# Linear attention with a bilinear FFN on one core: pair scores by whole 128x128 blocks and the state update as a step of its own

## The chip, the cores and the metric

One core of one Trainium2 chip runs the whole program. The metric is the device time of one execution in microseconds (us). It is a little longer than the span that the profile shows, which runs from the first to the last instruction.

## What is computed

The reference cut to what matters (B=4, H=8, S=768, D=48; x has 3072 tokens of 384 features; d_ff=1024; all in float32 at the end):

```python
f = 1.0 / (1.0 + np.exp(-f_logit))
for t in range(S):
    state = f[:, :, t, :, None] * state + np.einsum('bhd,bhe->bhde', k[:, :, t], v[:, :, t])
    y[:, :, t] = np.einsum('bhd,bhde->bhe', q[:, :, t], state)
x = y.transpose(0, 2, 1, 3).reshape(B * S, H * D)
a = x @ w1
b = x @ w2
h = a * b @ w3
out = h @ w_out
```

The first part is a gated linear attention with a decay per feature, the second an FFN whose hidden layer is the product of two projections.

## The kernel before, in words

**Attention by chunks.** The sequence is cut into NU = 24 chunks of C = 128 tokens, six per batch entry (NCH = 6). A chunk has eight heads as four pairs (HP = 4): the two heads of a pair lie on partitions 0 to 47 and 64 to 111. For chunk u the gate is a sigmoid on ScalarE (L386). Two scans on VectorE make the running products forwards and backwards (L394, L416), and q and k are scaled by them into Q (L410) and K (L431 and L432; the second writes the two halves of 64 tokens of every second pair in swapped places, and v is loaded in three transfers, L349 and L351, so that its rows fit).

**Pairs** (L457, and L445 for the first four chunks): K^T Q per head gives a 128x128 block of scores, laid into the PSUM tile pa. From chunk 4 (NPE = 4) a block is made on 64x64 tiles of the array: the 64 early keys against all 128 queries, and the 64 late keys against the 64 late queries. The quarter in which every key is later than every query isn't computed. There are 16 matmuls in a chunk and 32 instructions, since a float32 matmul is two. The first four chunks use 8 matmuls of 128x128 (16 instructions). ScalarE copies pa into the tile A (L542, three copies in a chunk; L539, one copy, in the first four). GpSimd zeroes what lies beyond the diagonal by affine_select (L548: four selects of 64x256 in a chunk, one of 128x1024 in the first four). In chunks 4 and 5 it also clears the quarters that nothing writes (L559, L560).

**Values** (L490): v^T A per head, into pa again from chunk 4. **Update** (L522): K^T of the chunk, turned by PE transposes (L467, PSUM tile pk) and copied (L567), times v. It isn't made for the last chunk of a batch entry ("closes": 5, 11, 17, 23). VectorE adds the result to the state S (L611 to L617) and ScalarE spreads it into sb (L625). **State** (L509): sb^T Q added onto the values, not for the first chunk of an entry ("opens": 6, 12, 18). From chunk 4 these three make one step of PE: values, update, state, in that order. For the first four chunks, update is a step of its own.

**y.** ScalarE copies y out with its sum (L635). From chunk 4 it is written to memory by features in two transfers (L655) and read back as x^T in one (L658). The first four chunks are permuted on PE instead (L663).

**Weights and FFN.** The weights come as 64-bit words and are turned to float32 on ScalarE and VectorE (L1079 to L1096). w3 and w_out are folded into one matrix on PE (L1143, copied out at L1150). Six blocks of 512 tokens go through the FFN (L685). Its two products use seven multiplications in place of eight on half matrices, with sums on VectorE (L755, L809 to L827, L921 to L970).

**Order of the work.** Nothing is scheduled by the compiler. A planner (class Plan, L74) holds tasks with an engine, a cost, dependencies and a priority. It takes again and again the task that can start first (ties by priority) and so fixes the order of each engine's instructions. Attention from chunk 4 has priorities of n0 - 1000 (pairs), - 999 (turn), - 998 (values), - 997 (update), far ahead of the FFN, and each such PE task adds a slack of 0.8 to what it waits for on another engine. A dependency across engines adds a lag of 0.2. FFN tasks cost 0.43 to 1.33 in the plan, and folds 5.15. PSUM banks of the FFN are five named tiles (plan.pool "f"), taken as they come free. Loads go through moves (L334), which counts each transfer on SP (0.45) and at most eight outstanding ones ("lane").

Of the kernel before, what the change touches and what calls it, by code (L numbers as in the profile page):

```python
# [73 lines left out]
class Plan:  # L74


    def __init__(self):
        self.tasks = []
        self.slots = {}
        self.pools = {}  # L80
        self.got = None

    def slot(self, name, n):

        self.slots[name] = [n, []]

    def pool(self, name, n):

        self.pools[name] = [None] * n
# [11 lines left out]
    def order(self):  # L101
# [6 lines left out]
        def after(t, ds):  # L108

            if any(d["end"] is None for d in ds):  # L110
                return None
            return max([0.0] + [d["end"] + (d["lag"] + t["slack"] if d["eng"] != t["eng"] else 0.0) for d in ds])

        def places(t, name):

            ends = [(after(t, enders[id(h)]) if h else 0.0, i) for i, h in enumerate(self.pools[name])]
            return [e for e in ends if e[0] is not None]

        def start(t):

            waits, at = list(t["deps"]), free.get(t["eng"], 0.0)
            for name in t["takes"]:
                if name in self.pools:
                    ends = places(t, name)
                    if not ends:
                        return None
                    at = max(at, min(ends)[0])
                    continue
                n, taken = self.slots[name]
                if len(taken) >= n:  # L130
                    waits += enders[id(taken[-n])]
            ready = after(t, waits)
            return None if ready is None else max(at, ready)

        while left:
            at, _, _, t = min(
                ((at, t["prio"], t["no"], t) for t in left if (at := start(t)) is not None), key=lambda x: x[:3]
            )
            t["at"], t["end"] = at, at + t["cost"]
            free[t["eng"]] = t["end"]  # L140
            for name in t["takes"]:
                if name in self.pools:
                    t["got"] = min(places(t, name))[1]
                    self.pools[name][t["got"]] = t
                else:
                    self.slots[name][1].append(t)
            left.remove(t)
            done.append(t)
# [57 lines left out]
def ranged(ctx, tc, q, k, f_logit, v, w1, w2, w3, w_out, out, ident, w12, wc, left):  # L206
# [14 lines left out]
    ps_f = ctx.enter_context(tc.tile_pool(name="ps_f", bufs=1, space=PSUM))  # L221
# [5 lines left out]
    masked = [keep.tile([P, 2, HP, C], F32, name=f"A{i}") for i in range(2)]  # L227
# [34 lines left out]
    plan.pool("f", NF)  # L262
    plan.slot("a", 2)
    plan.slot("lane", 8)
# [4 lines left out]
    def bank():  # L269

        return ps_f.tile([P, TB], F32, name=f"f{plan.got}")

    def idle(n):

        to = ps_f.tile([P, TB], F32, name=f"f{NF - 1}")[:, 0:TH]
# [58 lines left out]
    def moves(n, size, rate, emit, deps, prio, late=0.0):  # L334


        for j in range(n):
            i = plan.add("SP", 0.45, (lambda: None) if j else emit, [d] if j else deps, prio - j * 1e-3, takes=["lane"], lag=0.6)
            d = i
            t = plan.add("DMA", size / n / rate, lambda: None, [i], prio - j * 1e-3, lag=1.3 + late, frees=[i])  # L340
        return t

    def loaded(dst, u):

        if u < NPE:
            nc.sync.dma_start(dst, v[u])
            return
        to, of = (t.rearrange("p (b two m) -> p b two m", two=2, m=2 * D) for t in (dst, v[u]))
        nc.sync.dma_start(to[:, :, 0], of[:, :, 0])  # L349
        for a in (0, 64):  # L350
            nc.sync.dma_start(to[a : a + 64, :, 1], of[64 - a : P - a, :, 1])  # L351

    def front(u):

        s, t = st[u], tk[u]
        n0 = need(u)

# [13 lines left out]

        t["lf"] = moves(2, 197, 250, load(fu, f_logit), free(2, "g"), n0 - 30)
        t["lk"] = moves(2, 197, 250, load(ku, k), free(2, "k"), n0 - 29.5)
        t["lq"] = moves(2, 197, 250, load(qu, q), free(3, "q"), n0 - 29)

        def load_v():
            s["v"] = at(12288 + NQ, DM) if u == 3 else loads.tile([P, DM], F32, name="vt")
            loaded(s["v"], u)

        t["lv"] = moves(  # L380
            1 if u < NPE else 3, 197, 320, load_v, [] if u == 3 else past(u, 4 if u in (4, 5, 6) else 3, "v", "s"),
            n0 - (28.2, 28.2, 28.2, 29.6, 12)[min(u, NPE)],
        )
# [5 lines left out]
        if u % NCH and "d" in tk[u - 1]:  # L389
# [32 lines left out]
        def scale_k():  # L422
            s["K"] = work.tile([R, NQ], F32, name="K")
            if u < NPE:
                nc.vector.tensor_tensor(s["K"], ku, s["R"], ALU.mult)
                return

            kk, k_, r_ = (
                x.rearrange("p (b two h c) -> p b two h c", two=2, h=2, c=C // 2) for x in (s["K"], ku, s["R"])
            )  # L430
            nc.vector.tensor_tensor(kk[:, :, 0], k_[:, :, 0], r_[:, :, 0], ALU.mult)  # L431
            nc.vector.tensor_tensor(kk[:, :, 1, ::-1], k_[:, :, 1], r_[:, :, 1], ALU.mult)  # L432

        t["k"] = plan.add("DVE", 0.7 if u < NPE else 0.8, scale_k, [t["r"], t["lk"]] + past(u, 2, "a", "t"), n0)
# [3 lines left out]
    def pairs(u):  # L438
        s = st[u]
        s["pa"] = ps.tile([P, 2, NQ], F32, name="pa")  # L440
        if u < NPE:
# [7 lines left out]
            return  # L449

        for hp in range(0, HP, 2):
            for late in range(2):
                for swap in range(2):
                    a = (hp + swap) * C
                    h0 = 64 * (late ^ swap)
                    for par in range(2):
                        nc.tensor.matmul(  # L457
                            s["pa"][h0 : h0 + 64, par, a + 64 * late : a + C],
                            lhsT=s["K"][rows(par), a + h0 : a + h0 + 64],
                            rhs=s["Q"][rows(par), a + 64 * late : a + C], start=True, stop=True,  # L460
                        )

    def turn(u):
        s = st[u]
        s["pk"] = ps.tile([P, HP, R], F32, name="pk")
        for hp in range(HP):
            nc.tensor.transpose(  # L467
                out=s["pk"][:, hp], in_=s["K"][:, hp * C : hp * C + C],
                identity=ident[0:R, 0:R],
            )  # L470

    def y_block(u, b):
        py = st[u]["py"]
        return py[:, b] if u < NPE else py[0:R, b // 2, b % 2 * C : b % 2 * C + C]

    def values(u):
        s = st[u]
        opens = u % NCH == 0
        if u < NPE:
            s["py"] = bank().rearrange("p (h c) -> p h c", c=C)[0:R]  # L480
        else:
            s["py"] = ps.tile([P, 2, NQ], F32, name="pa")
        met_ = set()
        for hp in heads_of(u):
            for par in range(2):
                h = 2 * hp + par
                half, b = side(u, hp, par)
                w = 64 if half == 0 else D
                zone = (half, 0 if u < NPE else par)
                nc.tensor.matmul(  # L490
                    y_block(u, b)[64 * half : 64 * half + w], lhsT=s["v"][:, h * D : h * D + w],
                    rhs=s["A"][:, par, hp], start=zone not in met_, stop=opens, skip_group_check=True,
                )
                met_.add(zone)

    def from_state(u):
        s = st[u]
        if u % NCH == 0:
            return
        for hp in heads_of(u):  # L500
            if u < NPE:
                nc.tensor.matmul(
                    y_block(u, hp), lhsT=sb[(u - 1) % 2][:, hp], rhs=s["Q"][:, hp * C : hp * C + C],
                    start=False, stop=True, skip_group_check=True,
                )
                continue
            for par in range(2):
                half, b = side(u, hp, par)
                nc.tensor.matmul(  # L509
                    y_block(u, b)[rows(half)], lhsT=sb[(u - 1) % 2][rows(par), hp, rows(par)],  # L510
                    rhs=s["Q"][rows(par), hp * C : hp * C + C], start=False, stop=True,
                    skip_group_check=True,
                )

    def update(u):
        s = st[u]
        s["pd"] = ps.tile([P, HP, R], F32, name="pk")[0:R, :, 0:D]
        for hp in range(HP):
            for par in range(2):
                h = 2 * hp + par  # L520
                w = 64 if par == 0 else D
                nc.tensor.matmul(  # L522
                    s["pd"][64 * par : 64 * par + w, hp], lhsT=s["kt"][:, hp, 64 * par : 64 * par + w],
# [1044 lines left out]
```

## Time and profile before

| | us |
|---|---|
| median of 3 runs (lowest to highest) | 499.08 (499.04 to 499.2) |
| the profiled execution, its own time | 499.08 |
| its span | 497.2 |
| PE busy | 484.9 |
| VectorE busy | 362.1 |
| ScalarE busy | 166.8 |
| GpSimd busy | 69.7 |
| mean granted TensorE clock | 0.998 |

The rows of the trace give the start of an instruction (or of a run of like instructions), its length, its engine and line, the tiles as out<-in, and in brackets how long the engine had been idle and what ended that. Matmuls overlap in the array, so the time that one costs is the distance from its start to the start of the next, not its own length. The times of the rows count from the start of the span. The stages are: chunks 0 to 3 and the start (0 to 36 us), the first FFN block, the weights and the fold (to 135 us), chunks 4 to 23 among FFN work (83 to 314 us), and the rest of the FFN (to 494 us).

### The profile page before, as it was taken

To read this page: it belongs to the slowest core of one execution; us is meant where nothing else is said; L and a number is where in the kernel's file an instruction comes from. 1 tells how busy PE (TensorE), PEld (TensorE's weight loads), DVE (VectorE), ACT (ScalarE), POOL (GpSimd) and SP (SyncE) were. 2 spreads that over 40 slices of the span, in tenths; PEclk is the share of its full clock that TensorE was granted. 3 is DMA by queue.
4 is the path that set the end of the run, shared out by engine and by line. 5 is a ranking of instruction groups with operands and counts; after the bars stand their busy time and mean duration, and the time that the engine had idled before them with its cause. 6 is when DMAs were issued, how large, how long until landed. Compare 5 with 4: busy or idle time off the path is not lost.

```text
span 497.2 us, 9542 instructions
## 1 busy us (share of the span) xinstructions
PE 484.9 (98%) x3698; PEld 407.6 (82%) x3698; DVE 362.1 (73%) x721; ACT 166.8 (34%) x380; POOL 69.7 (14%) x115
## 2 busy tenths in 40 slices
PE   8889999999999999999999999999999999999995
PEld 6778745655799888889888888998899888889994
DVE  7998899989989677878677965446673667664541
ACT  4688456662433444443334443101100111101000
POOL 9210000432212111123212221000000000000000
PEclk9999999999999999999999999999999999999999
DMA  6889377563335554344532203100021000000011
GB/s 177 293 301 280 98 248 257 194 180 96 96 98 142 153 147 100 99 120 138 139 86 74 55 18 82 48 33 0 2 63 49 16 1 0 1 0 2 32 55 48
DMA packets 44789, 49.99 MB, mean 101 GB/s; under 512 B 15296, under 2 KB 34240, under 8 KB 43712
## 3 DMA queue, kind: packets, MB, share of 16 engines
q1 hardware_dynamic: 44736, 49.30, 33.3%
q8 instruction: 31, 0.51, 0.4%
q14 instruction: 22, 0.18, 0.1%
HBM read 40.63 MB, written 8.65 MB: 99 GB/s over the span
## 4 chain that ended last, share of the span: by engine, by line
PE 76%; POOL 1%; DVE 0%; ACT 0%; issue 0%
PE f L685 61%; PE pa L490 4%; PE f L1143 3%; PE pa L457 3%; PE pa L509 2%; PE pk L467 2%; PE pk L522 1%; POOL A L548 0%; ACT ys L635 0%; DVE place L949 0%; DVE o L970 0%; POOL A L560 0%; POOL A L559 0%; DVE nil L1202 0%; DVE zero L1200 0%
## 5 line engine op out<-in xcount | busy, mean ns | idle before, releaser
L685 PE MATMUL f<-xt,w 128*128 128x256 f32 (+1 forms) x600 | 158.5, 396 | 0.0
L685 PEld LDWEIGHTS f<-xt,w 128*128 128x128 f32 x600 | 113.6, 190 | 24.9 <-issue 11.2
L685 PE MATMUL f<-place 128*128 128x192 f32 (+1 forms) x504 | 112.6, 350 | 0.0
L685 PEld LDWEIGHTS f<-place 128*128 128x128 f32 x504 | 87.5, 190 | 6.1 <-DVE place L809 0.5
L548 POOL TENSOR_SCALAR_AFFINE_SELECT A<-A 64x256 f32<-64x256 f32 (+1 forms) x84 | 57.2, 701 | 239.2 <-PE pk L467 104.3
L1143 PE MATMUL f<-place 128*128 128x384 f32 x128 | 43.1, 490 | 0.6 <-ACT wc L1150 0.6
L788 ACT COPY a<-f 128x256 f32<-128x256 f32 x36 | 13.4, 372 | 77.4 <-PE f L685 67.2
L685 PE MATMUL f<-xt,place 128*128 128x256 f32 x144 | 37.7, 385 | 0.0
L1143 PEld LDWEIGHTS f<-place 128*128 128x128 f32 x128 | 23.8, 190 | 17.0 <-ACT wc L1150 1.2
L685 PE MATMUL f<-wc,ab 128*128 128x192 f32 x192 | 35.4, 327 | 0.0
L685 PEld LDWEIGHTS f<-wc,ab 128*128 128x128 f32 x192 | 31.9, 190 | 0.7 <-issue 0.4
L394 DVE TENSOR_TENSOR_SCAN fwd<-gate,floor 112x512 f32<-112x512 f32 x24 | 29.7, 1237 | 2.6 <-ACT gate L386 2.1
L416 DVE TENSOR_TENSOR_SCAN bwd<-gate,back 112x512 f32<-112x512 f32 x24 | 29.4, 1226 | 0.7
L812 DVE TENSOR_TENSOR place<-f,a 128x256 f32<-128x256 f32 x36 | 15.2, 423 | 20.2 <-PE f L685 20.2
L685 PEld LDWEIGHTS f<-xt,place 128*128 128x128 f32 x144 | 26.4, 189 | 4.0 <-issue 0.4
L542 ACT COPY A<-pa 64x256 f32<-64x256 f32 (+1 forms) x60 | 24.3, 439 | 13.9 <-PE pa L457 13.3
L635 ACT ACTIVATE ys<-pa 112x512 f32<-112x512 f32 x20 | 11.9, 597 | 49.9 <-PE pa L509 45.7
L490 PEld LDWEIGHTS pa<-A,vt 128*64 128x64 f32 (+1 forms) x320 | 17.6, 129 | 7.8 <-issue 5.5
L490 PE MATMUL pa<-A,vt 128*64 128x128 f32 (+1 forms) x320 | 22.7, 280 | 1.0 <-POOL A L560 1.0
L1079 ACT ACTIVATE place<-place 128x512 f32<-128x512 f32 (+2 forms) x24 | 21.2, 884 | 3.5 <-DVE w L1096 2.0
L685 PE MATMUL f<-place,w 128*128 128x256 f32 x72 | 21.6, 382 | 0.0
L1082 ACT ACTIVATE place<-place 128x512 f32<-128x512 uint32 (+2 forms) x24 | 21.1, 885 | 0.0
(117 smaller groups left out, 638.6 us busy)
## 6 DMA issues: line engine op xcount, KB each, us to landing
place<-in_w_dram SPq DMA_DIRECT2D x8, 1024.0 KB, 4.8
place<-in_w_dram SPq DMA_DIRECT2D x12, 512.0 KB, 9.3
out_dram<-o SPq DMA_DIRECT2D x24, 192.0 KB, 1.9
q<-in_q_dram SPq DMA_DIRECT2D x46, 96.0 KB, 2.4
f<-in_f_logit_dram SPq DMA_DIRECT2D x44, 96.0 KB, 2.4
k<-in_k_dram SPq DMA_DIRECT2D x44, 96.0 KB, 2.3
yt<-ys SPq DMA_DIRECT2D x40, 96.0 KB, 2.2
xt<-yt SPq DMA_DIRECT2D x20, 192.0 KB, 2.9
```

Of the source, the lines that this page charges most:

```text
L394: nc.vector.tensor_tensor_scan(s["P"], gate[u % 2][:, 0:NQ], floor, 0.0, ALU.mult, ALU.max)
L416: nc.vector.tensor_tensor_scan(s["R"][:, ::-1], gate[u % 2][:, NQ:0:-1], back[:, ::-1], 0.0, ALU.mult, ALU.max)
L457: nc.tensor.matmul(s["pa"][h0 : h0 + 64, par, a + 64 * late : a + C], lhsT=s["K"][rows(par), a + h0 : a + h0 + 64], rhs=s["Q"][rows(par), ...
L490: nc.tensor.matmul(y_block(u, b)[64 * half : 64 * half + w], lhsT=s["v"][:, h * D : h * D + w], rhs=s["A"][:, par, hp], start=zone not in ...
L542: nc.scalar.copy(parts_of(s["A"].rearrange("p r h c -> p (r h c)"))[p0:p1, :, f], parts_of(s["pa"].rearrange("p r n -> p (r n)"))[p0:p1, : ...
L548: nc.gpsimd.affine_select(out=a, in_=a, pattern=pattern, compare_op=ALU.is_ge, fill=0.0, base=0, channel_multiplier=-1,)
L685: nc.tensor.matmul(out_, lhsT=lhs[i], rhs=rhs[i], start=start and i == 0, stop=i == len(lhs) - 1, skip_group_check=True,)
L788: nc.scalar.copy(q["a"], q["X"])
L812: nc.vector.tensor_tensor(ups["u3", k], q["Y"], q["a"], ALU.add)
L1079: nc.scalar.activation(m, hi.bitcast(F32), AF.Abs)
L1082: nc.scalar.activation(lo.bitcast(F32), lo, AF.Copy, bias=2.0, scale=2.0**-51)
L1143: nc.tensor.matmul(w3s["p", jc], lhsT=w3s[jc][:, kc * P : kc * P + P], rhs=wos[:, kc], start=(kc == 0), stop=(kc == KF - 1),)
```

## The change

From chunk 4 on, the pairs are made as in the first four chunks: eight matmuls of 128x128 in place of sixteen on 64x64 tiles, with one copy on ScalarE in place of three, one select on GpSimd in place of four, and no clearing. K is scaled in one instruction in its natural order, and v is loaded in one transfer in place of three. The state update is again a PE task of its own (cost 0.6, priority n0 - 997), and values with state another. In the planner, the banks "f" are a ring of five taken in turn and not named tiles, a transfer's limit of eight outstanding ones is gone, loads are one task each, the load of v has an earlier priority, and two waits of FFN tasks are moved (takes_ab to c11, got to got0 in down). The FFN's instructions and the way of y through memory (L655, L658) are the same on both sides.

```diff
-        self.pools = {}
-        self.got = None
...
-        def places(t, name):
-
-            ends = [(after(t, enders[id(h)]) if h else 0.0, i) for i, h in enumerate(self.pools[name])]
-            return [e for e in ends if e[0] is not None]
...
-    ps_f = ctx.enter_context(tc.tile_pool(name="ps_f", bufs=1, space=PSUM))
+    ps_f = ctx.enter_context(tc.tile_pool(name="ps_f", bufs=NF, space=PSUM))
...
-    plan.pool("f", NF)
+    plan.slot("f", NF)
     plan.slot("a", 2)
-    plan.slot("lane", 8)
...
-    def moves(n, size, rate, emit, deps, prio, late=0.0):
-
-
-        for j in range(n):
-            i = plan.add("SP", 0.45, (lambda: None) if j else emit, [d] if j else deps, prio - j * 1e-3, takes=["lane"], lag=0.6)
-            d = i
-            t = plan.add("DMA", size / n / rate, lambda: None, [i], prio - j * 1e-3, lag=1.3 + late, frees=[i])
-        return t
+    def moves(issue, size, rate, emit, deps, prio, late=0.0):
+
+        i = plan.add("SP", issue, emit, deps, prio, lag=0.6)
+        return plan.add("DMA", size / rate, lambda: None, [i], prio, lag=1.3 + late)
...
-            loaded(s["v"], u)
-
-        t["lv"] = moves(
-            1 if u < NPE else 3, 197, 320, load_v, [] if u == 3 else past(u, 4 if u in (4, 5, 6) else 3, "v", "s"),
-            n0 - (28.2, 28.2, 28.2, 29.6, 12)[min(u, NPE)],
-        )
+            nc.sync.dma_start(s["v"], v[u])
+
+        t["lv"] = moves(0.45, 197, 320, load_v, [] if u == 3 else past(u, 4 if u in (4, 5, 6) else 3, "v", "s"), n0 - (28.2, 28.2, 28.2, 29.6, 27)[min(u, NPE)])
...
-            kk, k_, r_ = (
-                x.rearrange("p (b two h c) -> p b two h c", two=2, h=2, c=C // 2) for x in (s["K"], ku, s["R"])
-            )
-            nc.vector.tensor_tensor(kk[:, :, 0], k_[:, :, 0], r_[:, :, 0], ALU.mult)
-            nc.vector.tensor_tensor(kk[:, :, 1, ::-1], k_[:, :, 1], r_[:, :, 1], ALU.mult)
+            nc.vector.tensor_tensor(s["K"], ku, s["R"], ALU.mult)
...
-        for hp in range(0, HP, 2):
-            for late in range(2):
-                for swap in range(2):
-                    a = (hp + swap) * C
-                    h0 = 64 * (late ^ swap)
-                    for par in range(2):
-                        nc.tensor.matmul(
-                            s["pa"][h0 : h0 + 64, par, a + 64 * late : a + C],
-                            lhsT=s["K"][rows(par), a + h0 : a + h0 + 64],
-                            rhs=s["Q"][rows(par), a + 64 * late : a + C], start=True, stop=True,
-                        )
...
+        t["a"] = plan.add("PE", 1.1, pairs, [t["q"], t["k"]] + past(u, 1, "y" if u > NPE else "m"), n0 - 1000, slack=slack)
+
+        def taken():
+            s["A"] = work.tile([P, 2, HP, C], F32, name="A")
+            nc.scalar.copy(s["A"].rearrange("p r h c -> p r (h c)"), s["pa"])
+
+        t["m"] = plan.add("ACT", 1.1, taken, [t["a"]] + past(u, 2, "v"), n0)
...
+        t["c"] = plan.add("POOL", 1.2, causal, [t["m"]], n0)
+
+        if not closes:
...
+            t["t"] = plan.add("PE", 0.45, turn, [t["k"]] + past(u, 1, "d"), n0 - 999, slack=slack)
...
-            def value():
-                values(u)
-                if not closes:
-                    update(u)
-                from_state(u)
-
-            t["v"] = t["s"] = plan.add(
-                "PE", 1.2 + 0.35 * (not closes) + 0.5 * (not opens), value,
-                [t["c"], t["lv"]] + past(u, 0, "e") + past(u, 1, "y", "b", "d"), n0 - 998, slack=0.8,
-            )
...
+        t["v"] = plan.add(
+            "PE", 1.05 if opens else 2.1 if u < NPE else 1.6, value, [t["c"], t["lv"]] + past(u, 1, "y", "b"),
+            n0 - 998, takes=["f"] if u < NPE else [], slack=slack,
+        )
...
+            t["s"] = plan.add("PE", 0.6, update, [t["e"], t["lv"]] + past(u, 1, "d"), n0 - 997, slack=slack)
...
-            begin = takes_ab(jc, plan.add("PE", 0.0, lambda: None, ready + [s["S", 3]] + old(1, "m7"), n0))
-            pe("m1", one_, m1, [begin], 0, takes=["f"])
+            pe("m1", one_, m1, ready + [s["S", 3]] + old(1, "m7"), 0, takes=["f"])
...
-                q["c11"] = plan.add("ACT", 0.38, c11, [q["m2"]], -200, frees=[q["m1"]])
+                q["c11"] = takes_ab(jc, plan.add("ACT", 0.38, c11, [q["m2"]], -200, frees=[q["m1"]]))
...
-            pe("m1", m1, got + old("m7"), takes=["f"])
+            pe("m1", m1, got0 + old("m7"), takes=["f"])
```

## The prediction

> **What bounds the kernel now.** I read the page first: busy time, then the waits, then the chain that ended last, in order of time, and last the timeline of PE with its neighbours.
>
> ```profile
> PE 484.9 (98%) x3698; PEld 407.6 (82%) x3698; DVE 362.1 (73%) x721; ACT 166.8 (34%) x380; POOL 69.7 (14%) x115
> ```
>
> TensorE (PE) is busy for all but 12.3 us, and most of those lie in the first 36 us (latency of the first chunks) and after 494 us (the last stores). A busy PE isn't PE at its peak, so I check with the distances between matmuls: from 36.66 us on, matmuls of one shape follow each other at one constant step (8 of 128x192 in 1.30 us below), and PE loses only a few waits. So whatever PE issues more from chunk 4 on lengthens the run by as much, whatever it issues less shortens it, and what ScalarE, VectorE, GpSimd or the DMAs save counts only where PE waits for it. The chain shows what one chunk costs:
>
> ```profile
> 155.17 0.83 PE pa L457 x32
> 156.00 0.54 PE pk L467 x4
> 156.53 5.21 PE f L685 x30
> 161.74 1.06 PE pa L490 x12
> 162.80 0.41 PE pk L522 x13
> 163.21 0.58 PE pa L509 x16
> 163.79 2.79 PE f L685 x14
> ```
>
> Start, length, line: pairs 0.83, turn 0.54, FFN as a filler, then values, update and state in one block of 1.06 + 0.41 + 0.58 = 2.05, and FFN again. (Some matmul records are merged away, so the counts are low. The times aren't.)
>
> **Pairs.** The new form runs in the first four chunks of this same execution:
>
> ```profile
> 9.03 1.16 PE L445 MATMUL pa<-Q,K 48*128 48x128 f32 x16
> 10.12 0.67 PE L522 MATMUL pk<-vt,kt 128*64 128x48 f32 x16
> 10.71 2.43 PE L277 MATMUL f<-floor 112*128 112x256 f32 x10
> ```
>
> From start to start, 8 pairs matmuls of 48x128 (16 instructions) take 10.12 - 9.03 = 1.09 us, and the three other chunks give 1.09 too. Against 0.83 that is +0.26 in each of the 20 chunks from 4 on: **+5.2 us**. Nothing hides it, since PE is what is full.
>
> **Update as a step of its own.** Here it takes 10.71 - 10.12 = 0.59 and not the 0.41 that it adds inside the block. What the array pays for a change from FFN matmuls to the attention's and back is in these rows:
>
> ```profile
> 146.25 1.46 PE L685 MATMUL f<-wc,ab 128*128 128x192 f32 x8
> 147.55 1.46 PE L685 MATMUL f<-place 128*128 128x192 f32 x8
> 148.85 1.46 PE L685 MATMUL f<-place,ab 128*128 128x192 f32 x8
> 150.25 1.13 PE L490 MATMUL pa<-A,vt 128*64 128x128 f32 x16
> 152.30 1.57 PE L685 MATMUL f<-wc,place 128*128 128x192 f32 x8
> 153.70 1.46 PE L685 MATMUL f<-wc,ab 128*128 128x192 f32 x8
> ```
>
> Eight of these take 1.30 (147.55 to 148.85), but 1.40 ahead of the values (148.85 to 150.25) and 1.40 again as the first ones behind them (152.30 to 153.70): 0.10 in, 0.10 out, 0.20 for each separate block. Chunks that make no update show values and state alone: 1.06 + 0.58 (chain, 183.25 and 249.50 us). So a chunk with an update costs, against 2.05 now: about 2.05 where the planner sets the update just ahead of the values (the same shapes in another order, +0); 1.06 + 0.58 + 0.59 = 2.23 where just behind (+0.18); and 1.06 + 0.58 + 0.59 + 0.20 = 2.43 where FFN work lies between (+0.38). By the plan's own numbers the update can start 0.2 + 1.1 + 0.55 + 0.2 + 0.8 = 2.85 us after the pairs (the copy of A, then that of kt, on ScalarE), the values 0.2 + 1.1 + 0.2 + 1.2 + 0.2 + 0.8 = 3.7 after them (copy, select). FFN tasks of 0.43 to 1.33 set the places between, and the turn may come earlier than the pairs now that it no longer follows the values of the chunk before. I can't tell which of the three cases will be most frequent, so I weigh them 0.35, 0.25 and 0.4: 0.25 x 0.18 + 0.4 x 0.38 = 0.20 a chunk. 16 chunks of the 20 have an update: **+3.2 us**, with 0 and 16 x 0.38 = 6.1 as ends.
>
> **Copy, select, clearing.** A chunk's three copies take 1.24 us in a row on ScalarE, the one copy of the first chunks 1.01 (L539). Four selects of 681 ns on the mean give 2.7 us, one of 128x1024 takes 1.11 on the mean. This matters at two places only:
>
> ```profile
> 91.21 4.51 POOL L548 TENSOR_SCALAR_AFFINE_SELECT A<-A 64x256 f32<-64x256 f32 x4 [61.10 <-issue]
> 96.12 0.31 POOL L560 MEMSET A<- 64x256 f32 x1
> 96.48 1.19 PE L490 MATMUL pa<-A,vt 128*64 128x128 f32 x16 [0.66 <-POOL A L560]
> 110.50 1.19 PE L490 MATMUL pa<-A,vt 128*64 128x128 f32 x16 [0.35 <-POOL A L560]
> ```
>
> In chunks 4 and 5 PE stood idle for 0.66 and 0.35 until GpSimd had selected and cleared. With one select and no clearing A is ready about 90.04 + 0.1 + 1.0 + 1.1 to 3 = 92 to 94, ahead of the end of the fold at 95.7: **-1.0 us**. In the chunks after these, FFN work covers the select, and a shorter one gains nothing.
>
> The long select could hurt VectorE:
>
> ```profile
> 12.18 1.09 POOL L548 TENSOR_SCALAR_AFFINE_SELECT A<-A 128x1024 f32<-128x1024 f32 x1
> 12.27 1.54 DVE L425 TENSOR_TENSOR K<-k,bwd 112x512 f32<-112x512 f32 x1
> ```
>
> K took 1.54 beside this select and 0.69 elsewhere, 0.85 more. A rule speaks against the change here: by the Trainium skill, "SBUF — State Buffer", section "Who interferes with whom", GpSimd and VectorE share one port pair under an exclusive lock held for a whole instruction, so one long select may block VectorE's two-input operations for its full length, where a short one lets them in between. By that rule alone, with VectorE as the bound, 20 chunks would lose up to 20 x 1.1 = 22 us, an estimate. I take 0: the four short selects hold VectorE back as well, and between 150 and 200 us VectorE is busy for 40.2 of 50 us and PE for 50.0, so a VectorE that is 0.85 late is caught up. Without that cover the row gives at most 20 x 0.85 = 17 us.
>
> **The rest.** One K instruction of 0.69 stands for two that together take 0.67 from start to next start (140.71 to 141.38): 0. v comes in one transfer for three, which takes two issues a chunk off SP. No values matmul waits for a DMA in the list of waits, so the gain is 0, and VectorE's waits for x^T bound what a worse order of the transfers could cost now that the plan doesn't count eight of them: two waits, 4.4 us in all (DVE L755), 0 of which reach PE today. Taken 0, ends 0 and +4.4. A ring of banks instead of named ones makes a task wait for the oldest bank. In both FFN forms the banks are freed in the order in which they were taken, so I take 0. The nearest wait is PE's 0.6 for a fold's bank (L1143 on L1150), and one of these in each of six blocks would be +3.6. The first 36 us have the same instructions in nearly the same order: 0, with its PE waits of 1.41 at 30 us and 0.8 at 14 us as the ends of a luckier or worse order (-1.5 to +1.5).
>
> **Sum.** 5.2 + 3.2 - 1.0 = +7.4 us on the profiled execution, which took 499.08 us around a span of 497.2; that is also the median of the runs. **Forecast: 506.5 us**, own range 504 to 509.5.
>
> **Rivals.**
> - *New PE waits* (509.5 to 515 us, at 511.6 with 6.1 in place of 3.2 for the updates and half of the 4.4 for the transfers): the plan now knows less of transfers, and its shorter attention loop presses more of VectorE's work into less time. For it: VectorE is over 80% busy where attention runs. Against it: PE shows no such wait between 125 and 300 us, and a slower PE gives VectorE more room.
> - *Only the pairs count* (501.5 to 504 us, at 502.8: 5.2 - 1.0, and -0.5 from the start): updates lie next to the values nearly always. For it: both become ready within 0.85 us. Against it: the update no longer waits for the values' select.
> - *Faster than before* (under 498.1): the shorter chain through ScalarE and GpSimd, 0.2 + 1.6 us less a chunk, pulls PE's waits out. Its place is PE's idle time in the attention stage. It would have to be worth more than 5.2 us. All the waits that I find, from the 0.8 and 1.41 at the start through 0.6 at a fold and 1.0 in chunks 4 and 5 to 0.3 at the last check, are 4.1 us. Removing every one of them gives 499.08 + 5.2 - 4.1 = 500.2, so it decides only if the plan also packs the blocks closer than now. I see nothing that would.
> - *It doesn't do what its title says*: y's three transfers a chunk (L655 twice, L658) stand on both sides of the diff, so nothing comes from there either way. Then the terms above are all there is, and the forecast stays.
>
> **Chances.** Forecast's case 0.58, new waits 0.22, only the pairs 0.14, within 0.2% (a measurement of this kernel can't tell less from no change) 0.03, faster 0.03. So faster 0.03, same 0.03, slower 0.94. The range reaches into both neighbouring cases: 502 to 512.
>
> **What would show it.** L-rows for pairs with 48*128 in all chunks, 1.09 from start to start; update rows of 0.59 with FFN on both sides or next to values; no clearing on GpSimd, 24 selects, and no PE wait for GpSimd at 96 and 110 us; the stage from 317 us on as long as before (some 180 us). I am wrong if the FFN tail changes its length, if PE shows waits of its own between 125 and 314 us, or if the first FFN matmul moves far from 36.66 us.

## The result and the profile after

The changed kernel takes 504.25 us (median of four runs, 504.02 to 505.59) against 499.14 us for the kernel before on the same chip (499.04 to 499.23). The ratio is 1.0108, with a 95% interval of 1.009 to 1.0126: about 1% slower. The profiled execution took 504.48 us around a span of 502.7.

The page of the changed kernel, busy time by engine:

```profile
PE 493.0 (98%) x3378; PEld 411.3 (82%) x3378; DVE 364.1 (72%) x701; ACT 162.1 (32%) x340; POOL 43.7 (9%) x51
```

GpSimd lost 26 us of work and ScalarE 4.7, and the run became longer all the same, because TensorE (PE) got 8.1 us more and still has no room. The chain of waits that ended last (start, length, line; L388 is now the pairs, L414 the turn, L438 the values, L453 the state, L474 the update, L554 the FFN):

```profile
159.41 1.50 PE f L554 x8
160.91 0.59 PE pk L474 x14
161.50 1.49 PE f L554 x6
163.00 1.09 PE pa L388 x16
...
174.26 1.09 PE pa L388 x16
175.35 0.59 PE pk L474 x14
175.95 2.35 PE f L554 x10
178.30 0.39 PE pk L414 x4
178.69 1.31 PE f L554 x6
180.00 1.06 PE pa L438 x13
181.06 0.58 PE pa L453 x16
181.65 0.59 PE pk L474 x14
```

Pairs cost 1.09 where they cost 0.83. The update costs 0.59 where it cost 0.41 inside the block, and it stands in three places here: alone among FFN work (160.91), behind the pairs (175.35), and behind the state (181.65). The turn, which followed the pairs before, often stands by itself (178.30).

Chunks 4 and 5, where PE waited 0.66 and 0.35 us for GpSimd. PE first, then GpSimd:

```profile
88.54 5.34 PE L1011 MATMUL f<-place 128*128 128x384 f32 x16
93.81 1.13 PE L438 MATMUL pa<-A,vt 128*64 128x128 f32 x16
94.87 0.65 PE L453 MATMUL pa<-Q,sb 48*48 48x128 f32 x16
95.45 0.67 PE L474 MATMUL pk<-vt,kt 128*64 128x48 f32 x16
```

```profile
89.35 1.83 POOL L403 TENSOR_SCALAR_AFFINE_SELECT A<-A 128x1024 f32<-128x1024 f32 x1 [60.56 <-ACT A L397]
103.75 1.49 POOL L403 TENSOR_SCALAR_AFFINE_SELECT A<-A 128x1024 f32<-128x1024 f32 x1 [12.57 <-ACT A L397]
```

The first select ends at 91.18, and the values follow the fold of w3 and w_out at 93.81; those of chunk 5 start at 107.85, with the select done at 105.24. No wait stands ahead of the values any more.

The start of the FFN on PE moved:

```profile
29.33 1.13 PE L246 MATMUL f<-floor 112*128 112x256 f32 x4
...
32.37 2.84 PE L532 MATMUL f<-ys,ab 112*128 112x128 f32 x24
35.05 2.32 PE L554 MATMUL f<-xt,w 128*128 128x256 f32 x10
```

The first FFN matmul starts at 35.05 and not at 36.66, and the first fold at 76.37 and not at 77.98. These 1.6 us are a gain.

**Where the time went.** I add up the distances from start to start of PE's matmuls by kind, from the first FFN matmul to the last one, for both profiled executions:

| us | before | after | difference |
|---|---|---|---|
| first FFN matmul | 36.66 | 35.05 | -1.61 |
| pairs (20 chunks) | 16.58 | 21.84 | +5.26 |
| values (20) | 19.10 | 20.97 | +1.87 |
| update (16) | 8.71 | 9.42 | +0.71 |
| turn (16) | 7.07 | 6.78 | -0.29 |
| state | 9.93 | 9.93 | 0 |
| fold, with the waits in it | 44.35 | 42.60 | -1.75 |
| FFN | 348.96 | 349.99 | +1.02 |
| from the last matmul to the end of the span | 5.7 | 6.0 | +0.3 |
| sum | | | +5.5 |

The span grew by 502.7 - 497.2 = 5.5. The -1.75 are three waits that are gone: 0.71 and 0.40 for GpSimd, worked out from the starts, and 0.63 at the second fold.

### The profile page after: what moved, and what is told of

The parts are those of the page before. It is cut to its first block, busy times and chain, and to the rows that moved or that the text cites. A ratio compares the mean times of both kernels' runs of the same rounds, so it can differ in the third digit from the quotient of the medians.

```text
span 502.7 us, 8691 instructions
## 1 busy us (share of the span) xinstructions
PE 493.0 (98%) x3378; PEld 411.3 (82%) x3378; DVE 364.1 (72%) x701; ACT 162.1 (32%) x340; POOL 43.7 (9%) x51
## 2 busy tenths in 40 slices
DMA packets 36466, 49.94 MB, mean 99 GB/s; under 512 B 4416, under 2 KB 25920, under 8 KB 35392
## 4 chain that ended last, share of the span: by engine, by line
PE 95%; DVE 3%; DMA 0%; issue 0%; ACT 0%; POOL 0%; SPq 0%; DVEq 0%; ACTq 0%; POOLq 0%
PE f L554 69%; PE f L1011 8%; PE pa L388 5%; PE pa L438 4%; PE pk L474 2%; PE pa L453 2%; PE pk L414 2%; PE f L532 1%; DVE bwd L369 1%; DVE fwd L347 1%; PE f L446 1%; PE f L438 1%; DVE K L377 0%; DMA f<-in_f_logit_dram 0%; DVE Q L363 0%
## 5 line engine op out<-in xcount | busy, mean ns | idle before, releaser
L554 PE MATMUL f<-xt,w 128*128 128x256 f32 (+1 forms) x600 | 160.2, 398 | 0.0
L554 PEld LDWEIGHTS f<-xt,w 128*128 128x128 f32 x600 | 112.7, 190 | 25.1 <-issue 10.7
L554 PE MATMUL f<-place 128*128 128x192 f32 (+1 forms) x504 | 114.2, 351 | 0.0
L554 PEld LDWEIGHTS f<-place 128*128 128x128 f32 x504 | 87.4, 190 | 6.3 <-issue 0.6
L403 POOL TENSOR_SCALAR_AFFINE_SELECT A<-A 128x1024 f32<-128x1024 f32 x24 | 32.6, 1356 | 251.6 <-ACT A L397 251.6
L554 PE MATMUL f<-xt,place 128*128 128x256 f32 x144 | 37.6, 383 | 0.0
L554 PE MATMUL f<-wc,ab 128*128 128x192 f32 x192 | 35.3, 327 | 0.0
L397 ACT COPY A<-pa 128x1024 f32<-128x1024 f32 x24 | 24.3, 1013 | 28.4 <-PE pa L388 28.4
L347 DVE TENSOR_TENSOR_SCAN fwd<-gate,floor 112x512 f32<-112x512 f32 x24 | 31.1, 1294 | 2.5 <-ACT gate L339 1.7
L554 PEld LDWEIGHTS f<-wc,ab 128*128 128x128 f32 x192 | 32.0, 190 | 0.7 <-issue 0.2
L369 DVE TENSOR_TENSOR_SCAN bwd<-gate,back 112x512 f32<-112x512 f32 x24 | 30.8, 1283 | 0.7
L554 PEld LDWEIGHTS f<-xt,place 128*128 128x128 f32 x144 | 26.6, 189 | 3.9 <-issue 0.2
L388 PEld LDWEIGHTS pa<-Q,K 48*128 48x128 f32 x384 | 23.3, 187 | 7.7 <-issue 4.5
L388 PE MATMUL pa<-Q,K 48*128 48x128 f32 x384 | 27.9, 285 | 0.0
L363 DVE TENSOR_TENSOR Q<-q,fwd 112x512 f32<-112x512 f32 x23 | 16.7, 726 | 10.1 <-PE pa L453 10.1
L798 ACT COPY place<-f 128x192 f32<-128x192 f32 x12 | 3.8, 319 | 61.5 <-PE f L554 39.9
L438 PEld LDWEIGHTS pa<-A,vt 128*64 128x64 f32 (+1 forms) x320 | 17.5, 129 | 6.5 <-issue 6.4
```

Of the source, the lines that this page charges most:

```text
L347: nc.vector.tensor_tensor_scan(s["P"], gate[u % 2][:, 0:NQ], floor, 0.0, ALU.mult, ALU.max)
L363: nc.vector.tensor_tensor(s["Q"], qu, s["P"], ALU.mult)
L369: nc.vector.tensor_tensor_scan(s["R"][:, ::-1], gate[u % 2][:, NQ:0:-1], back[:, ::-1], 0.0, ALU.mult, ALU.max)
L388: nc.tensor.matmul(s["pa"][:, par, cols], lhsT=s["K"][rows(par), cols], rhs=s["Q"][rows(par), cols], start=True, stop=True,)
L397: nc.scalar.copy(s["A"].rearrange("p r h c -> p r (h c)"), s["pa"])
L403: nc.gpsimd.affine_select(out=a, in_=a, pattern=[[0, H], [1, C]], compare_op=ALU.is_ge, fill=0.0, base=0, channel_multiplier=-1,)
```

## The experiments

**The theory after the result:** pairs cost +5.26; the update on its own costs +3.3 (1.87 + 0.71 - 0.29 + 1.02 in the table); one select and no clearing gives 1.1 back; the start gives 1.6 and the second fold 0.6, which the prediction took for nothing. **The rivals:** the update costs by its place or by its change of shape; the gain at the start comes from the planner's new model of transfers, from v in one transfer, or from the moved update. Each kernel was timed beside the kernel before, which gave 499.08 to 499.17 in the three sessions.

**f_full: the pairs' part alone.** The kernel before, with the first four chunks' form in all chunks:

```diff
-        if u < NPE:          # in pairs, scale_k, taken, causal and the load of v
+        if True:
-            1 if u < NPE else 3, 197, 320, load_v, ...
+            1, 197, 320, load_v, ...
```

> The kernel before with the pairs alone changed: eight 128x128 matmuls, one copy, one select, no clearing, K and v in natural order; update stays inside the values' step, planner unchanged. My theory (PE issue decides): 20 x 0.26 = +5.2 us for the pairs, -1.0 for PE's waits in chunks 4 and 5, so +4.2, about 503.3 us. Rival 'new PE waits': more than +5.5, with idle rows on PE between 125 and 300 us. Rival 'the select chain pays it back': under +2.5.

Measured: 502.88 us (502.63 to 503.04), ratio 1.0076 (1.0062 to 1.009). The pairs take 21.85 in all (+5.27), the waits at 96 and 110 us are gone (-1.15 in the folds' sum), and the first FFN matmul stays at 36.64. So +5.27 - 1.15 is +4.1 on PE and +3.8 in the time; the FFN's own sum is 0.28 lower, and why stays open. The first and third terms of the prediction stand as they were put. v in one transfer alone, with the old model of transfers, moved nothing at the start.

**f_apart: the update as a step of its own, alone.**

```diff
-            values(u); update(u) unless closes; from_state(u)      # one PE task
+            values(u); from_state(u)                               # one PE task
+            t["s"] = plan.add("PE", 0.6, lambda: update(u), [t["e"], t["lv"]] + past(u, 1, "d"), n0 - 997, slack=0.8)
```

> The kernel before with the update alone made a task of its own (cost 0.6, priority n0 - 997); pairs stay on 64x64 tiles, planner unchanged. In the emitted order 9 updates stand right behind state, 2 behind pairs, 3 right ahead of values, 2 behind values of an opening chunk. My theory: 11 x 0.19 for a change of tile shape, about 0 for the other five, and 13 turns now stand apart from their pairs at 0.05 each: +2.7 us, about 501.8 us. Rival 'only the pairs count': within 0.7 us of before.

Measured: 502.46 us (502.27 to 502.57), ratio 1.0068 (1.0055 to 1.0082), so +3.4, 0.41 of which is one PE wait at 277 us. It is the prediction's second term: +3.2 in the sum, +3.0 here without that wait. My +2.7 for this run was too low; 0.2 of the difference are the three updates ahead of the values, which I had put at 0 and which cost 0.06 each by the next run.

**f_ahead: what a change of order costs without any FFN work between.** The kernel before, with update, values, state in one step in place of values, update, state.

```diff
-                values(u)
                 if not closes:
                     update(u)
+                values(u)
                 from_state(u)
```

> The kernel before with the update set ahead of the values inside the one step (update, values, state in place of values, update, state). The prediction's case 'just ahead of the values': +0 a chunk, 499.1 us. Rival: the order of the shapes matters, some 0.1 in each of 13 chunks, 500.4 us.

Measured: 499.71 us (499.3 to 499.84), ratio 1.0011 (1.0002 to 1.002): between the two expectations. The chain of f_ahead:

```profile
161.53 0.59 PE pk L522 x14
162.13 0.93 PE pa L490 x16
163.06 0.58 PE pa L509 x16
163.64 2.79 PE f L685 x14
```

0.59 + 0.93 + 0.58 = 2.10 against 1.06 + 0.41 + 0.58 = 2.05 in the kernel before. The chain sets the border between two steps of the same block where one ends last. By the starts the same blocks are 0.502 + 1.026 + 0.584 = 2.11 and 0.925 + 0.544 + 0.584 = 2.05, so update ahead of values costs 0.06 a chunk, 0.9 in 16. Another 0.3 are the wait for GpSimd in chunk 4, which moved into the block. The folds' sum fell by 0.73, because there the update now fills the time in which PE waited. So the prediction's "just ahead of the values, +0" should have been +0.06, from the change of shape alone.

**e1: the changed kernel with the pairs' part undone** (64x64 tiles, three copies, four selects, the clearing, three transfers of v; the moved update and the new planner stay).

```diff
+            if u >= NPE:
+                for hp in range(0, HP, 2): ...   # sixteen matmuls on 64x64 tiles
+                return
-            nc.sync.dma_start(s["v"], v[u])
+            loaded(s["v"], u)                    # three transfers from chunk 4 on
```

> The changed kernel with the pairs alone undone: 64x64 tiles, three copies, four selects, clearing in chunks 4 and 5, three transfers of v. My theory: 504.25 - 5.2 + 1.0 = 500.0 us. Rival 'new waits by the planner (ring of banks, transfers not counted)': then little of the loss goes with the pairs, and it stays above 501.5 us.

Measured: 500.87 us (500.11 to 501.83), ratio 1.0036 (1.0024 to 1.0048). This is 0.9 above my expectation. The first FFN matmul starts early (35.16), but the first fold doesn't (78.12): by the starts PE lost 0.89 at 52 us and 0.43 at 77 us. So something in the pairs' part is needed to keep the early start.

**g_v3: the changed kernel with nothing but v in three transfers** (of the natural order, the same bytes into the same places).

```diff
-            nc.sync.dma_start(s["v"], v[u])
+            if u < NPE: ...                                   # as it is
+            nc.sync.dma_start(to[:, :, 0], of[:, :, 0])       # heads 0, 1 and 4, 5
+            for a in (0, 64):                                 # the others, in two halves of the tokens
+                nc.sync.dma_start(to[a : a + 64, :, 1], of[a : a + 64, :, 1])
```

> The changed kernel with v of chunks 4 to 23 loaded in three transfers again (96 floats a piece, rows in natural order); nothing else differs. Theory formed after the runs above: the three transfers of v for chunks 4 to 6 stand on SP ahead of the last two pieces of w1 and w2 and hold them up, so that PE waits in the first FFN block and the early start is lost: 505.3 to 506 us, with the first fold near 78.0 us and not at 76.4. Rival (my prediction): one or three transfers of v make no difference, 504.3 us.

Measured: 506.4 us (505.35 to 507.05), ratio to the kernel before 1.0144 (1.0129 to 1.0158), which is 2.15 us above the changed kernel's 504.25 and above the 505.3 to 506 that I had expected. The two kernels were timed in two sessions: by the ratios the difference is 1.8 us, with intervals that just don't meet (up to 1.0126, from 1.0129), and the profiled executions differ by 1.8 too. The first fold is at 77.93 and not at 76.37, and the folds' sum is 0.40 higher. What SP issues shows how. The changed kernel, SP's queue (start, length):

```profile
23.26 1.58 SPq L334 DMA_DIRECT2D vt<-in_v_dram  x2
27.14 0.33 SPq L928 DMA_DIRECT2D place<-in_w_dram  x1
...
32.02 0.35 SPq L928 DMA_DIRECT2D place<-in_w_dram  x1
...
42.60 0.39 SPq L928 DMA_DIRECT2D place<-in_w_out_dram  x1
```

The same stretch in g_v3:

```profile
25.04 0.68 SPq L338 DMA_DIRECT2D vt<-in_v_dram  x1
26.24 1.73 SPq L340 DMA_DIRECT2D vt<-in_v_dram  x2
28.73 0.55 SPq L338 DMA_DIRECT2D vt<-in_v_dram  x1
29.99 1.79 SPq L340 DMA_DIRECT2D vt<-in_v_dram  x2
32.76 0.34 SPq L934 DMA_DIRECT2D place<-in_w_dram  x1
...
46.59 0.40 SPq L934 DMA_DIRECT2D place<-in_w_out_dram  x1
```

SP issues v of chunks 4 and 5 in 1.58 us in the one kernel. In the other these two loads stretch from 25.04 to 31.78, and the weights behind come later: the next piece of w1 or w2 by 5.6 us, the second piece of w_out by 4.0. Of the 5.6 us, 1.8 lie already ahead of the first transfer of v (25.04 against 23.26), behind the same pieces of weights in both kernels; this part can't be put down to v.

ScalarE's waits for w_out between 36 and 82 us, in the changed kernel and then in g_v3 (total, times, longest):

```profile
ACT place L950 <- DMA place<-in_w_out_dram: 3.9, 2, 3.4
```

```profile
ACT place L956 <- DMA place<-in_w_out_dram: 5.7, 2, 4.9
```

And PE's waits in g_v3, where the changed kernel has none from 36 us to the first fold:

```profile
49.72 2.86 PE L560 MATMUL f<-xt,w 128*128 128x256 f32 x12 [0.16 <-ACT ab L597]
52.81 24.75 PE L560 MATMUL f<-xt,w 128*128 128x256 f32 x66 [0.24 <-ACT ab L597]
77.93 5.43 PE L1017 MATMUL f<-place 128*128 128x384 f32 x16 [0.37 <-DVE place L970]
```

PE waits for ScalarE's copies, which stand behind the conversions of w_out, and for the fold's weights. I had expected the last pieces of w1 and w2 to be what holds it up.

The page counts 36466 DMA packets, 4416 of them under 512 bytes, in the changed kernel, and 44786 with 15296 under 512 bytes in g_v3. A piece of v in three transfers is two heads of 48 floats, 384 bytes. The Trainium skill, "DMA: Bandwidth & Descriptors", section "Specifications", puts the smallest transfer that keeps the line rate at 512 bytes. The rows agree in direction. They don't separate the small packets from the number of issues.

**f_moves: the planner's new model of transfers alone.** The kernel before, with

```diff
-        for j in range(n):        # a task for each transfer, eight outstanding at most
-            ...
+        i = plan.add("SP", (0.45, 0.87, 1.35)[n - 1], emit, deps, prio, lag=0.6)
+        return plan.add("DMA", size / rate, lambda: None, [i], prio, lag=1.3 + late)
```

> The kernel before with the planner's model of transfers alone changed to the new one (a load is one task, no limit of eight outstanding); every instruction is the same, their order differs. In the first 36 us the emitted order has the turn of chunk 3 ahead of the values of chunk 2 and no filler matmuls at 30 us, as in the changed kernel. My theory after the two traces: the first FFN matmul comes 1.6 us earlier (35.05 against 36.65), and so does the end: about 497.5 us. Rival 'the early start is lost again at the folds, where VectorE delivers w3': 499 us. Rival 'the limit of eight was needed': slower than 500 us.

Measured: 500.44 us (499.26 to 501.16), ratio 1.0024 (1.0015 to 1.0033). I had expected a gain, and it is a loss. The model brings the turn of chunk 3 ahead of chunk 2's values, and the first FFN matmul starts at 32.58, four us early (1.3 of them because half of the permutation of y, L659, now comes behind the first FFN matmuls). PE then waits for weights (idle time of PE and what ended it, f_moves):

```profile
54.63 5.85 PE L681 MATMUL f<-xt,w 128*128 128x256 f32 x16 [1.12 <-ACT ab L718]
60.92 16.57 PE L681 MATMUL f<-xt,w 128*128 128x512 f32 x38 [0.43 <-DVE w L1092]
79.13 5.11 PE L1139 MATMUL f<-place 128*128 128x384 f32 x15 [1.64 <-DVE place L1092]
```

The first fold ends up at 79.13, later than before the edit, and at 247.44 PE waits 0.66 more for VectorE. The early start is worth nothing here, since the weights aren't early too. The time is also that of the rival "the limit of eight was needed"; the edit takes out the limit and the task per transfer together, and no run separates them.

**g_moves_vlate: f_moves, with v of chunks 4 to 6 held back** until the plan has loaded the twelfth piece of weights, the last one of w1 and w2.

```diff
-            past(u, 4 if u in (4, 5, 6) else 3, "v", "s")
+            past(u, 4 if u in (4, 5, 6) else 3, "v", "s") + (asked[11:12] if u in (4, 5, 6) else [])
```

> The kernel before with the new model of transfers, and the three transfers of v for chunks 4 to 6 held in the plan until all twelve pieces of w1 and w2 are asked for. Theory: the early start of the new order is now kept, first fold near 76 us, so -1.6 us and perhaps also the 0.63 at the second fold: 496.8 to 497.6 us. Rival: the early start is lost at another piece of the weights, 499 us or more, as in the run with the new model alone (500.44).

Measured: 502.47 us (500.3 to 504.3), ratio 1.0061 (1.004 to 1.0082). The remedy made it worse, and it shows the mechanism best. SP, then ScalarE, then PE of g_moves_vlate:

```profile
40.37 0.39 SPq L1056 DMA_DIRECT2D place<-in_w_out_dram  x1
40.86 1.47 SPq L345 DMA_DIRECT2D vt<-in_v_dram  x1
...
48.45 1.26 SPq L347 DMA_DIRECT2D vt<-in_v_dram  x2
50.20 0.41 SPq L1056 DMA_DIRECT2D place<-in_w_out_dram  x1
```

```profile
55.73 0.88 ACT L1078 ACTIVATE place<-place 128x768 f32<-128x768 uint32 x1 [6.21 <-DMA place<-in_w_out_dram]
56.51 0.61 ACT L382 ACTIVATE gate<-f 112x512 f32<-112x512 f32 x1
57.02 0.35 ACT L718 COPY ab<-f 128x256 f32<-128x256 f32 x1
```

```profile
57.43 1.15 PE L681 MATMUL f<-xt,w 128*128 128x256 f32 x3 [3.64 <-ACT ab L718]
```

The held-back v now stands between the first two pieces of w_out. The second one is issued at 50.20 (47.42 in f_moves, 42.60 in the changed kernel). ScalarE stands for 6.21 us at the conversion of this piece, which nothing needs before the fold, and the copy L718, which the FFN needs at once, is behind it in ScalarE's order. PE loses 3.64 us. The profile names the copy as what PE waited for; the cause is two steps further back, in SP's queue.

**g_full_moves: pairs' part and new model together, update still inside.**

```diff
   # the edits of f_full and of f_moves on the kernel before
```

> The kernel before with both other parts of the change and without the third: pairs of 48x128 blocks with natural order, one copy, a long select and v in one transfer, and the planner's new model of transfers (which moves chunk 3's turn ahead of chunk 2's values); the update of the state stays inside the values' run. If v in one transfer is what lets the early start survive, the first FFN matmul comes near 35.0 us, the first fold near 76.4, and the time is that of the same kernel with the old model of transfers (502.9 us) less 1.6, so 501.3 us. If the early start is lost here too (first fold after 77.5 us), the time stays at 502.5 to 503.3 us, and the start of the changed kernel belongs to the moved update.

Measured: 501.4 us (500.41 to 501.58), ratio 1.0037 (1.0024 to 1.0051): the first expectation's time. The first fold starts at 76.78, 1.2 us earlier than in f_full. Not all went as expected: the FFN starts at 32.58 and not at 35.0, and PE waits for the fold's weights:

```profile
76.78 5.43 PE L1127 MATMUL f<-place 128*128 128x384 f32 x16 [1.38 <-DVE place L1080]
```

A start that is 2.5 us earlier than the changed kernel's (1.3 of them for the half of the permutation that comes later) gives no earlier fold: here the weights end the wait before the fold, while in the changed kernel PE doesn't wait before it at all. With f_full this gives a path through the change, each step from medians: 499.1, pairs' part +3.8, new model of transfers -1.5, the rest +2.85, which is 504.25. The rest is the moved update with the ring of banks, the earlier priority of v and the two moved waits of the FFN. The changed kernel with the update put back into the values' step wasn't tried, so this last step is a difference of two kernels from two sessions, and its parts aren't separated.

**g_vlate: the kernel before, with v of chunks 4 to 6 late** (the edit of g_moves_vlate on the kernel before).

> The kernel before with one edit: v of chunks 4, 5 and 6 is not asked for until the eleventh early piece of the FFN's weights has been asked for. If the three transfers of v hold up the weights in the kernel before as they do in the changed one, the first FFN matmul comes 1 to 1.6 us earlier than 36.65 and the time falls to 497.6 to 498.3 us. The rival: what ends the first 36 us in the kernel before is the turn of chunk 3 waiting for ScalarE, not the weights; the first FFN matmul stays at 36.6 us, late values only delay chunks 4 and 5, and the time is 499 to 500.5 us.

Measured: 499.23 us (498.62 to 499.37), ratio 1.0001 (0.9992 to 1.001). The rival holds: the first FFN matmul stays at 36.44. Three transfers of v aren't what bounds the kernel before; they cost something once the planner's new model has brought the start forward.

**f_clear: the gain of the third term by itself.** The kernel before, with the clearing as an early task of GpSimd's:

```diff
-            if u < NPE + 2:
-                nc.gpsimd.memset(a[0:64, :, 2], 0.0)
-                nc.gpsimd.memset(a[64:P, :, 0], 0.0)
+        if NPE <= u < NPE + 2:
+            plan.add("POOL", 0.65, cleared, past(u, 2, "v"), -50)   # the two memsets
```

> The kernel before with the clearing of A for chunks 4 and 5 as a GpSimd task of its own, long before it is needed. It takes away the 0.6 us that stand between the last select and the values there. Theory (PE's waits at 96 and 110 us are worth what they show, 0.71 + 0.40, and 0.6 us of each lie in the clearing): -0.6 - 0.4 = -1.0 us, about 498.1 us. Rival: PE then waits for something else at the same places, within 0.3 us of before.

Measured: 497.91 us (497.29 to 498.07), ratio 0.9974 (0.9964 to 0.9984): faster than both kernels. The values of chunks 4 and 5 in f_clear:

```profile
95.66 1.13 PE L490 MATMUL pa<-A,vt 128*64 128x128 f32 x16
...
109.25 1.13 PE L490 MATMUL pa<-A,vt 128*64 128x128 f32 x16
```

No wait stands behind either, and the selects are still four (4.50 us in chunk 4). So the 1.1 us that the change got back from GpSimd were to be had without it.

## Why the prediction was right, point by point

It forecast 506.5 us, slower by more than 0.2%; it is 504.25 and slower. Its own range, 504 to 509.5, holds the time near its lower end. The terms:

- **Pairs +5.2: right.** +5.26 in the changed kernel, +5.27 in f_full. The row of the first four chunks (1.09) held for all, and PE had nothing to hide it behind.
- **Update +3.2: right in size, by luck in its cases.** The four lines of the table give +3.3, and f_apart +3.4 with a wait of 0.41. I had given "just ahead of the values" a weight of 0.35 at +0. It never happens. Of the 16 updates 8 stand behind the state and 4 behind the pairs (a place that I hadn't listed), 2 alone, and 2 behind the values of an opening chunk, as before. In the 14 other chunks, values go from 0.925 to 1.062 and the update from 0.544 to 0.595 by the starts: 14 x 0.188 = 2.6, my +0.18. Two updates alone among FFN work add 2 x 0.10. What I left out is the turn: it left the pairs in 13 of 16 chunks, and 9 times it stands between FFN matmuls, where it takes 0.386 (once 0.581) in place of 0.439 but makes one more change to the FFN at 0.10: 9 x 0.05 = 0.4. Together 3.2, or 3.4 with the 0.2 of the one slow turn. The weights were wrong in both directions, the turn was left out, and the mean came out all the same.
- **Copy, select, clearing -1.0: right.** The two waits are gone, -1.1 by the starts, -1.15 in f_full. f_clear, where they are gone with four selects still there, shows that they go with the clearing alone.
- **The long select against VectorE, 0: right.** From chunk 4 on one K alone ran beside a select, and it took longer. The changed kernel:

```profile
165.27 1.09 POOL L403 TENSOR_SCALAR_AFFINE_SELECT A<-A 128x1024 f32<-128x1024 f32 x1 [8.93 <-ACT A L397]
...
165.90 1.00 DVE L377 TENSOR_TENSOR K<-k,bwd 112x512 f32<-112x512 f32 x1
```

K takes 1.00 here and 0.692 at the median. Between 125 and 300 us, engines in the order PE, PEld, DVE, ACT, POOL, first the kernel before and then the changed one:

```profile
125.00:300.00 175.00, 175.00 (x1853) 150.27 (x1849) 141.13 (x290) 70.95 (x189) 39.71 (x64) 1.00 0.40 105
```

```profile
125.00:300.00 175.00, 174.97 (x1620) 146.70 (x1618) 134.68 (x256) 67.34 (x155) 23.13 (x17) 1.00 0.37 103
```

VectorE is busy for 6.4 us less in this stretch, with 256 instructions in place of 290, and PE for all but 0.03 us. K isn't the only one to suffer: a scan beside a select takes up to 2.11 (1.22 at the median) and the product Q 1.58 once (0.68 or 0.69 elsewhere), and over the whole run VectorE is busy for 2.0 us more. The rule that the prediction weighed (the Trainium skill, "SBUF — State Buffer", section "Who interferes with whom") agrees in direction with these, and with the select, which takes 1.09 at the least and up to 2.11. The 22 us that I worked out from it don't show in the time: VectorE has 40 us of slack in this stretch.
- **"v comes in one transfer for three ... so the gain is 0", "the first 36 us ... 0": the step that failed.** v in one transfer is worth about 2 us in the changed kernel (g_v3: 2.15 by the medians, 1.8 between the profiled executions), and the start and the second fold gained 1.61 + 0.63. These are one gain and not two: f_full has v in one transfer and no early start, f_moves an early start and three transfers, and neither has a first fold ahead of 77.9. My reason was that no matmul of the values waits for a DMA. That is true and beside the point. I had priced v's transfers by who waits for v, and not by what is queued behind them on SP: pieces of weights, then ScalarE's conversions, then the FFN's copy or the fold. The bounds for the first 36 us, -1.5 to +1.5, missed -1.6 narrowly, and the bound for the transfers was put on one side only (0 to +4.4). I had also written that I would be wrong if the first FFN matmul moved far from 36.66; it moved by 1.6, and that is where the 7.4 predicted and the 5.4 measured in the profiled executions part: -1.6 at the start, -0.6 at the second fold, with +0.2 in all else.
- **The ring of banks, 0: nothing against it.** PE has no wait for a bank from 125 to 300 us. It wasn't tried alone.
- **The rivals.** No new PE waits came. "Only the pairs count" gave 502.8. f_full, the kernel with the pairs' part alone, takes 502.88, but that is partly luck: the rival's sum has -0.5 from the start, and in f_full the start doesn't move. "Faster" needed 5.2 us of waits to go, and there weren't that many.
- **One sign can't be read:** the last check, by which I meant to measure the FFN's tail, ran at 301.8 and not at 316.5, so the stretch behind it isn't the same work any more. The FFN's own sum is +1.02, at 46 runs of FFN matmuls in place of 35, or 0.09 for each further change of shape.

## What to carry to other kernels

Where one engine is busy all the time, count its instructions and its changes of shape: the pairs' term came out within 0.1 us, from a row of the old trace. Price a transfer also by what is issued behind it on its queue, and follow that through every engine that runs in order; the wait that the profile names may be two engines away from its cause. Before moving work to the bound engine to spare another one, look whether the wait can be had by doing the small thing earlier: two clearings moved forward gave 1.26 us, at no cost that the run shows.

## What the runs showed of the hardware

- **The 64x64 tiles kept what they left out.** They skip a quarter of the scores and took 0.829 us against 1.092, a ratio of 0.76, with twice as many matmuls. Three quarters of 1.092 would be 0.819, so the smaller tiles cost next to nothing of their own.
- **A change of shape has a price between attention steps too:** the same 16 matmuls of the values take 0.925 us between FFN work and an update, 1.026 between update and state, and 1.062 between FFN work and the state. From the FFN to a tiled step it is 0.09 to 0.10, and back 0.10.
- **The granted clock fell once, behind a long idle of PE.** In g_moves_vlate, which left PE idle for 3.64 us, the mean clock between 53 and 63 us is 0.83, and 0.69 in the 5.6 us behind the idle; in the changed kernel, with PE busy there, it is 1.00. Behind 1.64 us of idle in f_moves (79 us) it stayed at 1.00. So in g_moves_vlate PE went on at a lower clock behind the idle. One case shows it, and no run here shows where the limit lies.
